# Attention and feed-forward on one core: the first stage and the first chunk issued from a written list, with z in SBUF and the weight conversion's shifted word moved from PSUM to SBUF

## The chip, the cores and the metric

The kernel runs on one core of a Trainium2 chip. The metric is the device time of one execution in microseconds (us); less is better. The engines are called TensorE or PE (matrix products), VectorE or DVE, ScalarE or ACT, GpSimd or POOL, and SyncE or SP (which here only issues DMAs). Each works through its own instructions in order; between engines there are semaphores.

## What is computed

Attention with a window of 16 and with one summary key and value for each block of 32 positions, then a two-layer feed-forward part with ELU, all in fp32:

```python
B, H, S, D = 4, 8, 768, 64;  block, window = 32, 16;  nb = S // block      # 24 blocks
k_sum = k.reshape(B, H, nb, block, D).max(axis=3)
v_sum = v.reshape(B, H, nb, block, D).mean(axis=3)
scores_l = where(|i - j| < window, scale * q @ k.T, -1e9)
scores_s = scale * einsum('bhsd,bhnd->bhsn', q, k_sum) + log(block)
a = softmax(concatenate([scores_l, scores_s]))          # denominator + 1e-9
x = (a @ concatenate([v, v_sum])) as [3072, 512]
out = elu(x @ w_in) @ w_out                              # 512 -> 2048 -> 512
```

## The kernel before

Queries are handled in windows of 64 with their 96 neighbouring keys and the 24 summaries: 120 columns of scores. A *third* is 256 queries of one batch element, a *pair* two heads; a *unit* is one third of one pair, a *group* two units. The rows of x (3072) are taken in six chunks of 512. Every fp32 product of the feed-forward part is three products of split operands: x, the weights and the activations are each kept as a high part (fp32r) and the rest. Layer 1 of one of the 16 slices f of the hidden dimension is 12 products of 512 columns, layer 2 likewise 12; one f of one chunk is a *step* n, of 24 products.

The weights arrive as 64-bit floats and are converted on the chip, 32 tiles of 128x512, two for each step of chunk 0. `convert` has five instructions on three engines: POOL cuts the low word's top bits (L103), ACT rescales the high word into a PSUM tile `sh` (L108), DVE shifts and joins (L110, in place in `sh`) and puts the sign on (L113, into the SBUF tile `cv`, two buffers), ACT makes the high part (L117), POOL subtracts to get the rest (L118). The ELU is an exp on ACT (L597), a min and add on DVE in SBUF (L601), a max and add on DVE with one operand in PSUM (L602), the split's high part on ACT (L608) and its rest `gl` on POOL (L609).

`first_units` is the first stage: scores, softmax and values for the first two thirds of batch element 0, pair by pair, which give chunk 0 its x. `exp` there writes the sums z into free columns of the score banks; pairs 0 and 2, and 1 and 3, share banks (L284). The means of v are products with a matrix `mean` over the loaded windows and over a second load of the last rows, `rest` (`sums`); `spread` copies them to `vsx` and broadcasts them by two DMAs on ACT's queue into the rows of `v_t` that `vals` reads. Behind it the loop over the 16 steps of chunk 0 interleaves layer 1, the conversions of the next weights, the units of the following two thirds one by one (with block-diagonal queries `qbd`, their windows of k and v loaded again), and layer 2 of the step before. In both, the order of instructions on every engine is the order of the program (`manual_schedule` for all five). From chunk 1 on, units go in groups, with a period of four steps: scores and softmax in step 0, transposes in 1 and 2, values in 2; there only PE's and SP's order is the program's, and a planner orders the other engines. PSUM has banks o0 to o3 (layer 2's sums), h (two buffers, layer 1), a0 and a1 (attention, conversion).

Of the kernel before, what the change touches and what calls it, by code (L numbers as in the profile page):

```python
# [26 lines left out]
P = 128  # L27
# [7 lines left out]
NEG = -1.0e9  # L35


@with_exitstack
def attn_elu_ffn(ctx: ExitStack, tc: tile.TileContext, qT, kT, vT, v, w_in, w_out, out):
# [37 lines left out]
    todo, loads = list(order), list(order)  # L77
# [13 lines left out]
    def load_more(n):  # L91
        while loads and len(order) - len(loads) < n:
            load(loads.pop(0))

    def convert(tag="a1"):

        key = todo.pop(0)  # L100
        raw = raws.pop(key)
        lo_w, hi_w = raw[:, :, 0], raw[:, :, 1]
        nc.gpsimd.tensor_scalar(out=lo_w, in0=lo_w.bitcast(U8)[:, :, 3], scalar1=1 / 32, scalar2=-31 / 64,  # L103
                                op0=ALU.mult, op1=ALU.add)
        yield
        sh = psum.tile([P, WC], F32, tag=tag, name="sh")
        bits = sh.bitcast(U32)
        nc.scalar.mul(out=sh, in_=hi_w.bitcast(F32), mul=2.0 ** -112)  # L108
        yield
        nc.vector.scalar_tensor_tensor(out=bits, in0=bits, scalar=3, in1=lo_w,  # L110
                                       op0=ALU.logical_shift_left, op1=ALU.bitwise_or)
        cv = ffn.tile([P, WC], F32, tag="cv", name="cv", bufs=2)
        nc.vector.scalar_tensor_tensor(out=cv.bitcast(U32), in0=hi_w, scalar=0x80000000, in1=bits,  # L113
                                       op0=ALU.bitwise_and, op1=ALU.bitwise_or)
        yield
        w = wts.tile([P, 2, WC], F32R, tag=f"w{key[0]}_{key[1]}", name=f"w{key[0]}_{key[1]}")
        nc.scalar.copy(out=w[:, 0, :], in_=cv)  # L117
        nc.gpsimd.tensor_tensor(out=w[:, 1, :], in0=cv, in1=w[:, 0, :].bitcast(F32), op=ALU.subtract)  # L118
        weights[key] = w
# [21 lines left out]
    def normalize(sm, got, z=None):  # L141
        z = got if z is None else z
        nc.vector.tensor_scalar(out=z, in0=got, scalar1=1e-9, scalar2=None, op0=ALU.add)
        nc.vector.reciprocal(out=z, in_=z)  # L144
        nc.gpsimd.tensor_tensor(out=sm, in0=sm, in1=z.broadcast_to([P, UW, KC]), op=ALU.mult)  # L145

# [6 lines left out]
    def values(v_t, w0, pt, tag=None, o_ps=None):  # L153
        if o_ps is None:
            o_ps = psum.tile([P, UT], F32, tag=tag, name="o_ps")
        for t in range(UW):
            for h in range(2):
                nc.tensor.matmul(o_ps[h * D:(h + 1) * D, t * QW:(t + 1) * QW],
                                 v_t[0:KC, w0 + t, h * D:(h + 1) * D], pt[0:KC, t, h * QW:(h + 1) * QW],
                                 start=True, stop=True)  # L160
        return o_ps

# [4 lines left out]

    def take_x(o_ps, third, p):
        xh, xl = xs[third // 2]
        cols = slice(third % 2 * UT, (third % 2 + 1) * UT)  # L170
        nc.scalar.copy(out=xh[:, p, cols], in_=o_ps)  # L171
        nc.vector.tensor_tensor(out=xl[:, p, cols], in0=o_ps, in1=xh[:, p, cols].bitcast(F32), op=ALU.subtract)  # L172
# [12 lines left out]
    spares = {}  # L185

    def first_units():
# [6 lines left out]
        W2 = 2 * UW  # L194
        free = [f"w{i}_{f}" for f in range(NF - 1, 0, -1) for i in (2, 1)]

        def borrow(shape, name):
            return wts.tile(shape, F32, tag=free.pop(0), name=name)

        spares[0], spares[1] = free[0:4], free[4:8]  # L200
        sms = [borrow([P, 2, UW, KC], f"sm{p}") for p in range(NP)]
        pts = [borrow([P, 2, UW, P], f"pt{p}") for p in range(NP)]
        kn = [borrow([P, E + S], f"kn{p}") for p in range(NP)]
        qn = [borrow([P, 2, CH], f"qn{j}") for j in range(2)]
        rest = borrow([P, 2, row], "rest")
        mean = borrow([P, 2, 2 * BLK], "mean")
        vsx = borrow([P, NP, P], "vsx")
# [49 lines left out]
        for i in range(2):  # L257
            nc.gpsimd.memset(qbd[i], 0.0)

        for p in range(NP):  # L260
            nc.gpsimd.memset(kw[p][:, UW - 1, KB - E:KB], 0.0)
            nc.gpsimd.memset(vw[p][QW:KB, UW - 1, :], 0.0)

        src = v[0]
        nc.sync.dma_start(out=v_t[0][E:KB, 0, :], in_=src[0:KB - E, :])
        for w0, w1 in ((1, UW), (UW, W2)):
            windows = bass.AP(tensor=src.tensor, offset=src.offset + (w0 * QW - E) * row,
                              ap=[[row, KB], [QW * row, w1 - w0], [1, row]])
# [12 lines left out]
        def scores(p):  # L281
            q_p = qn[p // 2][:, p % 2]
            for h in range(2):
                banks_of[p, h] = psum.tile([P, UW * P], F32, tag=f"o{(2 * p + h) % NSUB}", name="s")  # L284
            views = [banks_of[p, h][:, 0:UW * KC].rearrange("p (t k) -> p t k", k=KC) for h in range(2)]
            for cols in (slice(0, KB), slice(KB, KC)):
                for w in range(W2):
                    for h in range(2):
                        rows, half = slice(h * D, (h + 1) * D), slice(w % 2 * QW, (w % 2 + 1) * QW)
                        right = kn[p][rows, w * QW:w * QW + KB] if cols.start == 0 else ks[rows, p, :]  # L290
                        nc.tensor.matmul(views[h][half, w // 2, cols], q_p[rows, w * QW:(w + 1) * QW], right,  # L291
                                         start=True, stop=True)
# [76 lines left out]
        for p in range(NP):  # L369
            put_maxima(0, p)  # L370
# [446 lines left out]
```

## Time and profile before

| | |
|---|---|
| time, median of 3 runs | 662.15 us (659.97 to 663.66) |
| time of the profiled execution | 663.22 us |
| its span in the profile | 661.5 us |
| mean granted TensorE clock | 0.971 of full |
| TensorE products, busy | 632.8 us (96%) |
| VectorE, ScalarE, GpSimd busy | 269.1, 275.2, 243.0 us |

The times are those of whole executions; the profile is of one of them. In rows of instruction groups, "x96" is the number of instructions, and a name after "<-" behind an idle time says what ended it. A matmul of fp32 operands (not fp32r) shows as two records. Durations of neighbouring products overlap, so the start-to-start distance is what one costs.

### The profile page before, as it was taken

To read this page: it belongs to the slowest core of one execution; us is meant where nothing else is said; L and a number is where in the kernel's file an instruction comes from. 1 tells how busy PE (TensorE), PEld (TensorE's weight loads), DVE (VectorE), ACT (ScalarE), POOL (GpSimd) and SP (SyncE) were. 2 spreads that over 40 slices of the span, in tenths; PEclk is the share of its full clock that TensorE was granted. 3 is DMA by queue.
4 is the path that set the end of the run, shared out by engine and by line. 5 is a ranking of instruction groups with operands and counts; after the bars stand their busy time and mean duration, and the time that the engine had idled before them with its cause. 6 is when DMAs were issued, how large, how long until landed. Compare 5 with 4: busy or idle time off the path is not lost.

```text
span 661.5 us, 11268 instructions
## 1 busy us (share of the span) xinstructions
PE 632.8 (96%) x4204; PEld 511.4 (77%) x4204; DVE 269.1 (41%) x858; ACT 275.2 (42%) x746; POOL 243.0 (37%) x260
## 2 busy tenths in 40 slices
PE   6685999999999999999999999999999999999997
PEld 4564887887888887788888887888888888888885
DVE  5547887773333452432343353332423323322222
ACT  5346765773442442533433434434524424322222
POOL 4317896984331332232322322313313313222221
PEclk8676999999999999999999999999999999999999
DMA  9649856941310441422015222311311000100001
GB/s 279 171 127 283 291 163 176 270 129 40 103 42 25 134 110 47 143 65 60 1 50 145 88 66 69 103 50 31 110 39 39 24 1 1 64 0 1 0 1 63
DMA packets 70606, 59.62 MB, mean 90 GB/s; under 512 B 29224, under 2 KB 62312, under 8 KB 70552
## 3 DMA queue, kind: packets, MB, share of 16 engines
q1 hardware_dynamic: 67024, 52.61, 27.3%
q10 hardware_dynamic: 3528, 6.29, 2.7%
q8 instruction: 33, 0.54, 0.3%
q14 instruction: 21, 0.17, 0.1%
HBM read 51.41 MB, written 6.29 MB: 87 GB/s over the span
## 4 chain that ended last, share of the span: by engine, by line
PE 87%; DVE 4%; DMA 2%; POOL 1%; ACT 1%; issue 1%; SPq 0%; ACTq 0%; DVEq 0%; POOLq 0%
PE o L619 38%; PE h L591 38%; PE t_ps L150 3%; PE o_ps L561 3%; PE s L537 2%; PE o_ps L313 1%; DVE cv L113 1%; DVE sh L110 1%; DVE sm L129 1%; POOL w L118 1%; DMA kn<-in_kT_dram 1%; PE s L291 1%; PE vsps L330 1%; DMA vxl<-vsx 1%; DMA out_dram<-ot 1%
## 5 line engine op out<-in xcount | busy, mean ns | idle before, releaser
L591 PE MATMUL h<-xh,w 128*128 128x512 f32 x760 | 256.3, 398 | 0.0
L609 POOL TENSOR_TENSOR gl<-e,gh 128x512 fp32r<-128x512 f32 x96 | 123.8, 1290 | 332.9 <-ACT gh L608 239.6
L619 PE MATMUL o<-w,gh 128*128 128x512 f32 x768 | 198.4, 397 | 1.3 <-ACT ot L640 1.0
L591 PEld LDWEIGHTS h<-xh,w 128*128 128x128 f32 x760 | 143.8, 189 | 30.5
L619 PEld LDWEIGHTS o<-w,gh 128*128 128x128 f32 x768 | 140.7, 188 | 33.4 <-ACT e L597 2.2
L591 PE MATMUL h<-xl,w 128*128 128x512 f32 x380 | 149.1, 392 | 0.0
L601 DVE TENSOR_SCALAR e<-e 128x512 f32<-128x512 f32 x96 | 46.5, 484 | 251.4 <-ACT e L597 251.2
L597 ACT ACTIVATE e<-h 128x512 f32<-128x512 f32 x96 | 57.3, 597 | 186.6 <-PE h L591 183.7
L619 PE MATMUL o<-w,gl 128*128 128x512 f32 x384 | 105.5, 390 | 0.0
L608 ACT CAST gh<-e 128x512 fp32r<-128x512 f32 x96 | 59.5, 620 | 104.8 <-DVE e L602 104.8
L619 PEld LDWEIGHTS o<-w,gl 128*128 128x128 f32 x384 | 72.0, 188 | 15.6 <-POOL gl L609 0.2
L591 PEld LDWEIGHTS h<-xl,w 128*128 128x128 f32 x380 | 72.1, 190 | 13.7
L137 ACT ACTIVATE sm<-sm,mx 128x120 f32<-128x120 f32 x192 | 73.5, 386 | 15.9 <-DVE mx L129 7.0
L602 DVE SCALAR_TENSOR_TENSOR e<-h,e 128x512 f32<-128x512 f32 x96 | 66.4, 692 | 3.3
L145 POOL TENSOR_TENSOR sm<-sm,z 128x480 f32<-128x480 f32 x48 | 47.4, 987 | 45.9 <-DVE z L144 43.8
L118 POOL TENSOR_TENSOR w<-cv,w 128x512 fp32r<-128x512 f32 x32 | 42.1, 1316 | 13.0 <-ACT w L117 12.2
L150 PE MATMUL t_ps<-ident,sm 128*120 128x128 f32 x192 | 31.9, 295 | 10.9 <-DVE mx L129 7.8
L129 DVE CUSTOM_DVE_ANT_0 sm<-s,mask 128x120 f32<-128x120 f32 x192 | 41.1, 277 | 0.2
L150 PEld LDWEIGHTS t_ps<-ident,sm 128*120 128x120 f32 x192 | 25.1, 147 | 17.6 <-POOL raw_w L103 6.9
L172 DVE TENSOR_TENSOR xl<-o_ps,xh 128x256 fp32r<-128x256 f32 x40 | 16.9, 423 | 51.6 <-ACT xh L171 51.6
L137 ACT ACTIVATION_READ_ACCUMULATOR sm<-sm,mx 128x1 f32 x192 | 35.1, 183 | 0.0
L171 ACT CAST xh<-o_ps 128x256 fp32r<-128x256 f32 x40 | 14.8, 371 | 38.0 <-PE o_ps L561 28.4
(89 smaller groups left out, 378.3 us busy)
## 6 DMA issues: line engine op xcount, KB each, us to landing
raw_w<-in_w_in_dram SPq DMA_DIRECT2D x16, 512.0 KB
raw_w<-in_w_out_dram SPq DMA_DIRECT2D x16, 512.0 KB
out_dram<-ot ACTq DMA_DIRECT2D x20, 256.0 KB
qbd<-in_qT_dram SPq DMA_DIRECT2D x16, 256.0 KB
kw<-in_kT_dram SPq DMA_DIRECT2D x28, 144.0 KB
vw<-in_v_dram SPq DMA_DIRECT2D x28, 144.0 KB
n<-in_kT_dram SPq DMA_DIRECT2D x16, 192.0 KB
n<-in_vT_dram SPq DMA_DIRECT2D x16, 192.0 KB
```

What stands on the lines that cost most here:

```text
L118: nc.gpsimd.tensor_tensor(out=w[:, 1, :], in0=cv, in1=w[:, 0, :].bitcast(F32), op=ALU.subtract)
L129: nc.vector.tensor_tensor_reduce(out=sm[:, t, :], in0=s_ps[:, t, :], in1=m, scale=-scale, scalar=3.0e38, op0=ALU.add, op1=ALU.min, accum_o ...
L137: nc.scalar.activation(out=sm[:, t, :], in_=sm[:, t, :], func=AF.Exp, bias=mx[:, t, :], scale=-1.0, accum_out=z[:, t, :])
L145: nc.gpsimd.tensor_tensor(out=sm, in0=sm, in1=z.broadcast_to([P, UW, KC]), op=ALU.mult)
L150: nc.tensor.transpose(t_ps[0:KC, t, :], sm[:, t, :], ident)
L591: nc.tensor.matmul(h_ps, w[:, a, cols], bb[:, cc, :], start=(k == 0), stop=(k == 3 * NCC - 1))
L597: nc.scalar.activation(out=e, in_=h_ps, func=AF.Exp)
L601: nc.vector.tensor_scalar(out=e, in0=e, scalar1=1.0, scalar2=-1.0, op0=ALU.min, op1=ALU.add)
L602: top = nc.vector.scalar_tensor_tensor(out=e, in0=h_ps, scalar=0.0, in1=e, op0=ALU.max, op1=ALU.add)
L608: nc.scalar.copy(out=gh, in_=e)
L609: nc.gpsimd.tensor_tensor(out=gl, in0=e, in1=gh.bitcast(F32), op=ALU.subtract)
L619: nc.tensor.matmul(o_acc[c][s], a[:, s * P:(s + 1) * P], w[:, bb, :], start=first and f == 0, stop=last and f == NF - 1)
```

## The change

- **A written order.** The first stage and chunk 0 are cut into small functions, and a string `FIRST` of some 750 words names them one by one with their arguments (`do[name](*numbers)`). An engine's instructions come in the order in which the words that use it stand in the list.
- **First stage.** z is an SBUF tile; scores go to (o0, o1), (o2, o3), (a0, a1), (o0, o1); local and summary scores are separate words (`sl`, `ss`). `rest` is no longer loaded: all twelve windows of v of batch element 0 are, the last four into `v_own`, and the sums run over twelve windows. `vals` uses the 96 window rows only, and `add_means` adds the means by one product for each head of a pair. The DMAs that remain for the means (`vm`, on SP) fill `v_own` alone. Single idle products on zeros (`idle`) stand between the scores and the first transposes.
- **Groups in chunk 0.** The units of chunk 0 go as groups 0 to 3. Groups 0 and 1 (the last third of batch element 0) read k, the maxima and v from the tiles of the first stage; groups 2 and 3 load their windows. The scores and softmax of group 4 are in the list too.
- **Conversion.** `sh` is gone: ACT rescales into `cv` in SBUF (two buffers), and both joins work there in place.
- **Chunk 0's products.** Layer 1 is issued in two parts (8 and 4 products), layer 2 in three parts of 4.
- **Chunks 1 to 4.** A group's values go into a bank of h; the next group's scores and softmax move from its step 0 to step 2 of the group before; mean products for the next batch element come after layer 2 of their step.

```diff
+FIRST = """
+    max.0 sl.0 ss.0 low.0.0 max.1 exp.0.0 sl.1 low.0.1 ss.1 max.2 exp.0.1 low.1.0 sl.2 low.1.1 ss.2 idle.1
+    exp.1.0 max.3 sl.3 exp.1.1 z.0.0 z.0.1 low.2.0 ss.3 idle.1 norm.0.1 low.2.1 norm.0.0 tr.0.1 z.1.0 exp.2.1
+    sums.0 z.1.1 norm.1.0 low.3.0 tr.0.0 norm.1.1 low.3.1 exp.2.0 ptc.0.1.0 w.0 ptc.0.0.0 sums.1 exp.3.0 z.2.1
+    tr.1.1 z.2.0 w.1 norm.2.0 tr.1.0 ptc.1.1.0 val.0 exp.3.1 z.3.0 q.0 ptc.1.0.0 norm.3.0 sums.2 z.3.1 tr.2.0
+    norm.3.1 spr.0.0 spr.1.1 w.2 spr.2.1 val.1 spr.3.1 vm ptc.2.0.0 X.0 tr.3.0 norm.2.1 M.0 add.0 w.3 ptc.3.0.1
+    S.0 X.1 tr.2.1 xh.0 add.1 ptc.2.1.1 xl.0 w.4 H.0 tr.3.1 xh.1 L.0 val.2 ptc.3.1.0 M.1 sk.0 xl.1 val.3 X.2 q.1
+    S.1 M.2 add.2 X.3 S.2 add.3 w.5 xh.2 H.1 xl.2 first.0 xh.3 L.1 H.2 xl.3 w.6 first.1 L.2 first.2 M.3 S.3 sk.1
+    first.3 X.4 gsc.0 E.0 H.3 ts.0 X.5 w.7 M.4 stt.0 L1h.1 L.3 glow.0.0 G.0 glow.0.1 ge.0.0 X.6 w.8 L1l.1 S.4
...
+    H.17 L.17 L1l.8 glow.2.0 H.18 L.18 mmul glow.2.1 E.8 q.3 L2a.7 ts.8 ge.2.1 X.20 stt.8 L2b.7 X.21 w.25 L2c.7
+    G.8 gz.2.1 ge.2.0 L1h.9 gl.8 w.26 gn.2.1 M.19 gz.2.0 L1l.9 M.20 S.19 gn.2.0 mact mm w.27 L2a.8 E.9 S.20 H.19
+    L2b.8 L.19 w.28 L2c.8 ts.9 H.20 stt.9 L.20 gtr.2.0 L1h.10 gpc.2.0.1 w.29 G.9 M.21 gl.9 S.21 L1l.10 w.30 pm.3
...
+"""
+        def low_bits(self):                                            # X
+            nc.gpsimd.tensor_scalar(out=self.lo, in0=self.lo.bitcast(U8)[:, :, 3], scalar1=1 / 32, scalar2=-31 / 64,
+                                    op0=ALU.mult, op1=ALU.add)
+        def exponent(self):                                            # M
+            self.cv = ffn.tile([P, WC], F32, tag="cv", name="cv", bufs=2)
+            nc.scalar.mul(out=self.cv, in_=self.hi.bitcast(F32), mul=2.0 ** -112)
+        def join(self):                                                # S
+            bits = self.cv.bitcast(U32)
+            nc.vector.scalar_tensor_tensor(out=bits, in0=bits, scalar=3, in1=self.lo,
+                                           op0=ALU.logical_shift_left, op1=ALU.bitwise_or)
+            nc.vector.scalar_tensor_tensor(out=bits, in0=self.hi, scalar=0x80000000, in1=bits,
+                                           op0=ALU.bitwise_and, op1=ALU.bitwise_or)
+        def high(self):                                                # H
+            nc.scalar.copy(out=self.w[:, 0, :], in_=self.cv)
+        def rest(self):                                                # L
+            nc.gpsimd.tensor_tensor(out=self.w[:, 1, :], in0=self.cv, in1=self.w[:, 0, :].bitcast(F32),
+                                    op=ALU.subtract)
-        sh = psum.tile([P, WC], F32, tag=tag, name="sh")
-        nc.scalar.mul(out=sh, in_=hi_w.bitcast(F32), mul=2.0 ** -112)
...
+        tags = {0: ("o0", "o1"), 1: ("o2", "o3"), 2: ("a0", "a1"), 3: ("o0", "o1")}
-            z = banks_of[p, h][:, UW * KC:UW * KC + UW].rearrange("p (t o) -> p t o", o=1)
-            zs[p, h] = exps(sms[p][:, h], mxs[p, h], z)
+            zs[p, h] = exps(sms[p][:, h], mxs[p, h])
+        def add_means(p):
+            for h in range(2):
+                nc.tensor.matmul(o_of[p][h * D:(h + 1) * D].rearrange("p w q -> p (w q)"),
+                                 vsx[KB:KC, p, h * D:(h + 1) * D],
+                                 pts[p][KB:KC, h].rearrange("p t q -> p (t q)"), start=False, stop=True)
...
-        o_ps = psum.tile([P, 2, UT], F32, tag="a0", name="o_ps")
+        o_of[g] = psum.tile([P, 2, UT], F32, tag="h", name="o_ps", bufs=2)
...
+            if step == 2:
+                if g < NG:
+                    group_values(g)
+                if g + 1 < NG:
+                    group_scores(g + 1)
+                if g < NG:
+                    group_high(g)
+                    group_rest(g)
+                if g + 1 < NG:
+                    for h in range(2):
+                        softmax(g + 1, h)
```

The words: `max` maxima of k, `low` masked scores with their minimum, `z` sum plus 1e-9 and reciprocal, `norm` POOL's multiply by it, `tr` transposes, `ptc` their copy (0 on DVE, 1 on ACT), `val` values, `add` add_means, `xh`, `xl` the split of x; `first` the parts of layer 1 of f = 0; `w`, `q`, `K`, `sk`, `sv` loads; `gsc`, `glow`, `ge`, `gz`, `gn`, `gtr`, `gpc`, `gval`, `gxh`, `gxl` the same for groups; `L1h`, `L1l`, `L2a` to `L2c` the parts of the layers; `E`, `ts`, `stt`, `G`, `gl` the ELU and its split.

## Rows read from the trace of the kernel before

**Rows 1.** The page: busy time of the engines (share of the span, instructions), and TensorE's busy tenths in 40 equal slices.

```profile
PE 632.8 (96%) x4204; PEld 511.4 (77%) x4204; DVE 269.1 (41%) x858; ACT 275.2 (42%) x746; POOL 243.0 (37%) x260
...
PE   6685999999999999999999999999999999999997
```

**Rows 2.** The timeline, lines of the first stage and of the starts of step 1 and of chunk 1: start, duration, engine, line, what it writes and reads, and in brackets the idle time before it and what ended it.

```profile
4.99 0.89 PE L291 MATMUL s<-kn,qn 64*64 64x96 f32 x32
...
8.26 0.40 ACT L137 ACTIVATE sm<-sm,mx 128x120 f32<-128x120 f32 x1 [5.04 <-DVE mx L129]
...
12.45 1.39 PE L291 MATMUL s<-kn,qn 64*64 64x96 f32 x27 [1.63 <-DVE z L143]
...
20.11 1.39 PE L291 MATMUL s<-kn,qn 64*64 64x96 f32 x27 [2.02 <-DVE z L143]
...
33.57 0.39 ACT L137 ACTIVATE sm<-sm,mx 128x120 f32<-128x120 f32 x1 [2.34 <-DMA vxh<-vsx]
...
37.14 1.13 PE L313 MATMUL o_ps<-pt,vxl 120*64 120x64 f32 x16 [1.01 <-DMA vxl<-vsx]
...
57.77 1.08 PE L150 MATMUL t_ps<-ident,sm 128*120 128x128 f32 x4 [6.71 <-DVE mx L129]
58.51 0.78 PE L591 MATMUL h<-xh,w 128*128 128x512 f32 x1
...
160.39 0.50 PE L591 MATMUL h<-xl,w 128*128 128x512 f32 x1
```

**Rows 3.** Windows: stretch (us), its length, busy time and instructions of PE, PE's weight loads, DVE, ACT and POOL, granted clock, DMA share, GB/s. The first two are chunk 0 from step 1 on and all that follows.

```profile
58.44:160.46 102.02, 100.90 (x579) 81.81 (x578) 73.43 (x164) 64.78 (x157) 82.32 (x83) 0.98 0.64 196
160.46:661.50 501.04, 495.19 (x3096) 400.80 (x3096) 164.08 (x559) 183.10 (x496) 136.84 (x121) 1.00 0.19 56
...
0.00:20.00 20.00, 11.41 (x206) 7.94 (x206) 12.70 (x73) 10.23 (x43) 8.26 (x36) 0.79 0.96 282
...
80.00:100.00 20.00, 20.00 (x115) 16.65 (x114) 17.12 (x43) 12.82 (x29) 18.26 (x20) 1.00 0.56 186
120.00:140.00 20.00, 20.00 (x125) 16.40 (x124) 16.24 (x43) 13.86 (x34) 18.90 (x20) 1.00 0.85 246
```

**Rows 4.** Windows of 4 us in the first stage, same columns: the granted clock stands third from the end.

```profile
20.00:24.00 4.00, 3.89 (x78) 3.50 (x82) 0.66 (x2) 1.79 (x8) 1.82 (x5) 0.50 0.95 225
24.00:28.00 4.00, 4.00 (x77) 3.36 (x70) 2.05 (x19) 1.81 (x8) 0.99 (x1) 0.50 0.64 198
28.00:32.00 4.00, 2.04 (x12) 1.55 (x12) 2.45 (x8) 0.51 (x2) 1.65 (x2) 0.90 0.03 8
...
48.00:52.00 4.00, 2.07 (x17) 1.70 (x15) 2.02 (x11) 3.08 (x11) 2.22 (x3) 1.00 0.23 41
```

**Rows 5.** Groups of instructions by line and shape in the first 58 us: busy time, mean ns of one, idle time before and what ended it.

```profile
L137 ACT ACTIVATE sm<-sm,mx 128x120 f32<-128x120 f32 x36 | 14.0, 392 | 13.9 <-DVE z L143 5.7 <-DVE mx L129 5.0 <-DMA vxh<-vsx 2.3
...
L225 PE MATMUL idle<-kw 128*128 128x480 f32 x4 | 3.6, 1048 | 1.5 <-DVE kn L230 1.5
```

**Rows 6.** DMA issues by line: what is written from where, count, size of one.

```profile
raw_w<-in_w_in_dram SPq DMA_DIRECT2D x16, 512.0 KB
...
n<-in_kT_dram SPq DMA_DIRECT2D x4, 384.0 KB
```

**Rows 7.** The chain of work that ended last, pieces of one group's period in chunk 2: start, us, what.

```profile
279.02 2.75 PE o L619 x12
...
288.51 2.72 PE h L591 x12
...
304.27 2.75 PE o L619 x12
```

**Rows 8.** Single lines: durations of one instruction in ns (shortest/median/longest), first and last start, form.

```profile
L113 DVE SCALAR_TENSOR_TENSOR cv<-raw_w,sh x32: 686/687/690, 36.9 to 148.2; 128x512 uint32<-128x512 uint32 x32
...
L601 DVE TENSOR_SCALAR e<-e x96: 418/427/1551, 57.5 to 652.0; 128x512 f32<-128x512 f32 x96
...
L488 DVE TENSOR_REDUCE ks<-n x4: 922/934/954, 61.2 to 109.4; 128x24 f32<-128x768 f32 x4
...
L144 DVE RECIPROCAL z<-z x48: 177/178/179, 10.4 to 550.2; 128x4 f32<-128x4 f32 x48
...
L118 POOL TENSOR_TENSOR w<-cv,w x32: 1269/1293/1580, 39.0 to 151.6; 128x512 fp32r<-128x512 f32 x32
```

**Rows 9.** The timeline, a POOL instruction and a DVE instruction that starts during it.

```profile
71.71 1.29 POOL L118 TENSOR_TENSOR w<-cv,w 128x512 fp32r<-128x512 f32 x1
...
71.93 1.36 DVE L601 TENSOR_SCALAR e<-e 128x512 f32<-128x512 f32 x1
```

**Rows 10.** Groups of instructions by line from 58.5 to 153.5 us: busy time, mean ns, idle time before.

```profile
L118 POOL TENSOR_TENSOR w<-cv,w 128x512 fp32r<-128x512 f32 x29 | 38.3, 1320 | 3.6 <-ACT w L117 2.8
...
L609 POOL TENSOR_TENSOR gl<-e,gh 128x512 fp32r<-128x512 f32 x15 | 19.4, 1296 | 6.2 <-ACT gh L608 5.6
L110 DVE SCALAR_TENSOR_TENSOR sh<-sh,raw_w 128x512 uint32<-128x512 uint32 x27 | 18.8, 695 | 11.3 <-ACT sh L108 6.3 <-POOL raw_w L103 2.8 <-POOL w L118 1.5
L113 DVE SCALAR_TENSOR_TENSOR cv<-raw_w,sh 128x512 uint32<-128x512 uint32 x27 | 18.6, 687 | 7.1 <-POOL w L118 5.1
L103 POOL TENSOR_SCALAR raw_w<-raw_w 128x512 uint32<-128x512 uint8 x26 | 17.4, 670 | 5.2 <-DMA raw_w<-in_w_out_dram 3.0
...
L145 POOL TENSOR_TENSOR sm<-sm,z 128x480 f32<-128x480 f32 x7 | 6.9, 988 | 0.0
```

More of the change, by code (lines that the diff above doesn't have):

```diff
@@ L151, in transposes @@
         return t_ps
[L153 to L161, printed above, removed]
     xs = {}
@@ L279, in maxima, with scores @@
                                     axis=AX.X, op=ALU.max)
-        def scores(p):
+        tags = {0: ("o0", "o1"), 1: ("o2", "o3"), 2: ("a0", "a1"), 3: ("o0", "o1")}
+        value_tags = ("o2", "o3", "o0", "o1")
+        sums_of, t_of = [], {}
+        def scores(p, part):
             q_p = qn[p // 2][:, p % 2]
[L283 to L292, printed above, removed]
@@ L371, in first_units @@
-        scores(3)
-        trans(1, 0, dve)
-        low(3, 0)
-        norm(2, 0)
-        exp(3, 0)
-        low(3, 1)
-        ps = sums()
-        trans(1, 1, dve)
-        norm(2, 1)
-        spread(ps)
-        one = convert(tag="a1")
-        next(one)
-        exp(3, 1)
-        trans(2, 0, dve)
-        norm(3, 0)
-        next(one)
-        trans(2, 1, act)
-        next(one)
-        norm(3, 1)
-        trans(3, 0, dve)
-        vals(0, "a0")
-        list(one)
-        take(0)
-        two = convert(tag="o2")
@@ L435, in load_group, with low, exp @@
-    def load_group(g):
+                    rows, half = slice(h * D, (h + 1) * D), slice(w % 2 * QW, (w % 2 + 1) * QW)
+                    right = ks[rows, p, :] if part else kn[p][rows, w * QW:w * QW + KB]
+                    nc.tensor.matmul(banks_of[p, h][half, w // 2, cols], q_p[rows, w * QW:(w + 1) * QW], right,
+                                     start=True, stop=True)
+        def low(p, h):
+            mxs[p, h] = lowest({0: 0}, banks_of[p, h], sms[p][:, h])
+        def exp(p, h):
+            zs[p, h] = exps(sms[p][:, h], mxs[p, h])
@@ new lines, in spread, with all_means, first @@
+        def spread(p, copy):
+            copy(out=vsx[KB:P, p, :], in_=sums_of[0][p * BLK:(p + 1) * BLK, :])
+        def all_means(queue, tile_, n):
+            src = vsx[KB:KC].rearrange("n p (o d) -> n o (p d)", o=1)
+            queue.dma_start(out=tile_[KB:KC, :, :], in_=src.broadcast_to([NS, n, row]))
+        layer = []
+        def first(part):
+            xh, xl = xs[0]
+            w = weights[(1, 0)]
+            if not layer:
+                layer.append(new_h(0))
+            todo_ = {0: [(cc, 0, x) for cc in (0, 1) for x in (xh, xl)], 1: [(2, 0, xh), (2, 0, xl)],
+                     2: [(cc, 1, xh) for cc in (0, 1, 2)], 3: [(3, 0, xh), (3, 1, xh), (3, 0, xl)]}[part]
+            for i, (cc, a, x) in enumerate(todo_):
+                nc.tensor.matmul(layer[0], w[:, a, cc * P:(cc + 1) * P], x[:, cc, :],
+                                 start=(part, i) == (0, 0), stop=(part, i) == (3, 2))
@@ new lines, in first_units @@
+        copies = (nc.vector.tensor_copy, nc.scalar.copy)
+        parts = (range(0, UW), range(UW, W2), range(W2, W2 + UW))
+        return {
+            "max": maxima, "sl": lambda p: scores(p, 0), "ss": lambda p: scores(p, 1), "low": low, "exp": exp,
+            "z": recip, "norm": norm, "tr": trans, "ptc": lambda p, h, i: take_t(p, h, copies[i]), "val": vals,
+            "add": add_means, "xh": take_h, "xl": take_l, "sums": lambda i: sums(parts[i]), "first": first,
+            "spr": lambda p, i: spread(p, copies[i]), "idle": idle,
+            "vm": lambda: [all_means(nc.sync, tile_, 2) for tile_ in v_own],
+        }
```

562 lines of the change are left out of this document (250 added, 312 removed).

## The prediction, made before the changed kernel was run

> **What bounds the kernel now.** I read the page first: TensorE (PE) is busy 96% of the span, and its slices are thin only at the start [rows 1]. Then stages: the first layer-1 product of step n=1 starts at 58.51 us, the first of chunk 1 at 160.4 [rows 2], so the span has three stretches: a first stage of 58.5, the rest of chunk 0 of 102, and chunks 1 to 5 of 501. In the second PE is busy 100.9 of 102.0, in the third 495 of 501 [rows 3]: both are set by PE's own work. The reader should see two more things. GpSimd (POOL) is nearly full beside PE while weights are converted, 18.3 and 18.9 of 20 us in two stretches [rows 3]; afterwards it idles. And the first stage has no full engine: there PE waits, for z to be read out of a score bank (1.63 and 2.02), for the means that go by DMA (1.01), and 6.71 before step 1; ScalarE (ACT) stands 2.34 behind its own DMA issue [rows 2]. TensorE's clock is at half there for long stretches [rows 4].
>
> **First stage.** The change takes away all four waits: z lies in SBUF, pair 2 has banks a0 and a1, the means are added by products of their own, so values need no DMA, and the last exps no longer stand behind DMA issues. What is left is ACT's chain. Eight softmaxes are four exps each, and an exp with its accumulator read takes 0.39 plus some 0.1 [rows 5]; before, four took 1.81 (8.26 to 10.07). From about 7.4 (the first low no longer stands behind the second maximum) eight take 14.5, to 22. VectorE's (DVE) work ahead of the last low is four maxima of 0.94, eight lows of 0.82 and some z, under 13 us from 4.65, so ACT sets it. Before, the last exp ended at 35.5. Behind 22 us PE has in its order a third of the sums, four transposes, three value sets, four adds and the twelve products of the first layer. At full clock: 0.9 + 4 x 0.36 + 3 x 1.1 + adds + 2.7; at half: 1.8 + 4 x 1.0 + 3 x 1.7 + adds + 4.8. No row has an add (24 rows deep, 512 columns, fp32, two halves); from 0.45, two records like those of the first layer, to 1.8, half of the two idle products that took 3.57 [rows 5]. I take 0.85 at full and 1.7 at half, since a pair's halves can run side by side as the small score products do. Sums: 11.7 and 22.5, so layer 1 of f=0 would end between 34 and 45. The clock rose at 28 after PE had been busy from 20 to 28 [rows 4]; the new order keeps PE supplied from 14 on, so it should rise part of the way: I take 40. The count n=1 then starts 18 us earlier.
>
> Hidden there: 48 instead of 40 mean products (eight more are 0.4 to 0.9 on PE, inside the wait for exps), the larger load of v (736 instead of 512 KB, under 1 us at the 282 GB/s of the first 20 us [rows 3]; the 4.8 MB of the first loads end near 18, before the third sums are due), the extra memsets (before the first scores). Without that cover each costs what it takes. The queue of SP holds its weights behind the two DMAs of means until about 27; w.3 then lands near 32 and is wanted at about 40. Loads still to come are some 22 MB: 29 weights of 512 KB, eight summaries of 384, four groups of queries and three of windows [rows 6]; at 186 to 282 GB/s [rows 3] they take 78 to 118 us, less than what follows.
>
> **Chunk 0 on PE.** Twelve products take 2.72 us [rows 7]. Fifteen steps are 15 x 5.44 = 81.6. A group of two units costs 25.25 - 8 x 2.72 = 3.5 [rows 7]: four are 14.0; the split scores of groups 0 and 1 add 0.8, group 4's early scores 1.0, the mean products 0.4. Sum 97.8, against the 102.0 there was. If PE still set the pace, chunk 1 would start at 40 + 98 + 2 = 140 instead of 160.4. Splitting layer 1 and layer 2 into parts adds no product.
>
> **Chunk 0 on the other engines.** One edit looks free and decides, I think: the conversion's shifted word moves from a PSUM bank (sh) to SBUF (cv). Before, each of the two join instructions had one operand in PSUM; now all operands of both lie in SBUF, and so do those of POOL's subtracts and multiplies. What the trace shows of DVE beside a busy POOL: every instruction with a PSUM operand keeps its time to the nanosecond (the second join 686/687/690); the ELU's first half, all in SBUF, spreads from 418 to 1551 [rows 8]. One of them starts 0.22 after a POOL subtract and ends 0.29 after that ends [rows 9]. POOL too has its stretched ones (the subtract's median is 1293, its longest 1580). So DVE and POOL exclude each other for some all-SBUF instructions. Not for all: reductions (922 to 954) and the reciprocal (177 to 179) never stretch [rows 8]. No DVE instruction of the trace reads two SBUF tensors. So the price of a join beside POOL lies between 0 (like the reduction) and full exclusion (like the ELU's first half). I take the latter: it is elementwise, the same 128x512 fp32, and the joins differ from the undisturbed rows by the lost PSUM operand alone.
>
> The Trainium skill, page "SBUF — State Buffer", section "Who interferes with whom", says that a DVE instruction with two SBUF inputs contends with a GpSimd instruction that reads SBUF, the later one blocked until the other ends; no run here shows that for two inputs. By it the sum below stands at its upper end; without it chunk 0 costs PE's 98.
>
> Exclusive time from 40 us on, by the durations of chunk 0 [rows 10]: POOL 27 low-bit instructions x 0.670 + 28 subtracts x 1.32 + 15 gl x 1.296 + 8 multiplies x 0.988 = 82.4; DVE 29 joins x (0.695 + 0.687) + 15 x 0.427 = 46.5. Together 129, well over PE's 98. Some of each instruction's head can hide behind the other's tail (0.43 ended 0.29 after POOL: 0.14 a handover, some 60 handovers, 9 us): 120. The other way, both engines work in a listed order, the subtract waits for the joins through ACT, and in some turns neither has work ready; a sixth more gives 150. I take 134, nearer the sum: about 9 us a step. In that list ACT stands behind late joins with its exps, and PE behind ACT; PE would be busy three quarters of the time, as in 44 to 52, where the clock stayed at full [rows 4]; if it fell, more is lost.
>
> **Sum.** Chunk 1 at 40 + 134 = 174 instead of 160.4: +13.6. Chunks 1 to 5: the same products except group 4's scores, -1.0. The profiled execution took 663.22 with a span of 661.5: 675.8. The median of the runs is 1.07 lower: 674.7, I say 675. Bounds: 35 + 120 gives 657, 45 + 150 gives 697.
>
> **Rivals.**
> - *No exclusion for two inputs; PE sets the pace.* For: reductions read SBUF undisturbed. Then -20.4 - 1.0: 642; with the first layer at 35 or 45, 636 to 648. It decides as soon as joins cost POOL less than about a quarter of their time: 82 + 6 + a quarter of 40 is 98.
> - *Faster, but held by cv's two buffers.* The buffer is now taken by ACT's multiply, before the joins, and given back by POOL's subtract: 0.63 + 1.38 + 0.62 + 1.32 = 4.0, two at once 2.0 for each conversion, where PE's pace leaves 3.25. With waits in three listed queues a life could reach 7, then 3.5 each, +8 over 30 conversions: 650.
> - *Chunks 1 to 4 lose.* Values now take one of the two h banks, and the next group's scores and exps come in the same step. If ACT took the eight exps (8 x 0.38) ahead of the copies, the bank would be free about 5.6 us after the scores, when the layer that wants it is due at 5.5. Two us late in 16 groups is 32: from 642 to 674; it decides above 1.3 a group. Against: the copies stand ahead of the softmax in the program.
>
> **Chances.** The forecast 0.62 (its own range 658 to 690), no exclusion 0.24, cv's buffers 0.08, the later loop 0.06. The runs before spread over 0.56%, so 0.5% (3.3 us) is what a measurement can tell from no change. Slower: 0.56 of the forecast and 0.05 of the last, 0.61. Same: 0.07. Faster: the two faster rivals and the forecast's lowest end, 0.32. Since cases of both signs hold most of the chance, the range spans both: 638 to 692 leaves out some 0.1 on each side.
>
> **What would show it.** Right: the first layer's products end near 40 (34 to 45) with no z or DMA waits; both joins spread above 0.69, up to about 2; POOL's subtracts too; chunk 1 starts at 165 to 185 with PE gaps in chunk 0 released by ACT, DVE or POOL; from there about 500 to the end. Wrong: joins at a flat 0.69, PE gapless from 40 to 140. The forecast also fails if POOL's order leaves DVE its turns only in POOL's idle time, or if the clock falls in the gaps.

## The result and the profile after

The changed kernel takes 663.97 us (median of 20 runs, 662.05 to 672.09), the kernel before beside it 661.50 (20 runs): a ratio of 1.0058, 95% interval 1.0031 to 1.0086. Slower, by 2.5 us where 13 were forecast. The profiled execution took 664.48, its span is 662.7. Five of the 20 runs took 671 to 672, at a mean granted clock of 0.972 to 0.974 where the profiled one has 0.984; none of the five was profiled.

Windows of the changed kernel, cut where its last product of the first layer of f=0 ends and where chunk 1 starts; columns as in [rows 3]:

```profile
0.00:38.82 38.82, 32.30 (x548) 21.54 (x548) 27.86 (x118) 22.38 (x82) 19.26 (x50) 0.96 0.87 265
38.82:166.94 128.12, 106.19 (x753) 82.39 (x753) 111.30 (x205) 71.15 (x177) 99.20 (x87) 0.93 0.50 158
166.94:662.70 495.76, 490.65 (x3069) 401.93 (x3067) 159.92 (x540) 179.90 (x488) 141.47 (x122) 1.00 0.19 55
```

And its timeline, the first products of step n=1 and of chunk 1:

```profile
40.08 0.50 PE L596 MATMUL h<-xh,w 128*128 128x512 f32 x1
...
166.94 0.39 PE L585 MATMUL h<-xh,w 128*128 128x512 f32 x1
```

Cut at these two starts, the three stretches were 58.5, 101.9 and 501.1 [rows 2]; now they are 40.1, 126.9 and 495.8: -18.4, +25.0 and -5.3, which is, up to rounding, the 1.2 between the two spans. A gain and a loss of some 20 us each stand behind a result near zero. In chunk 0 PE is busy 106 of 128 us where it was busy 100.9 of 102; POOL works 99, DVE 111.

Single lines of the changed kernel (shortest/median/longest ns), to be held against [rows 8]: both joins, the ELU's second half, which takes one operand from PSUM, its first half, which has one input, in SBUF, and POOL's two conversion instructions.

```profile
L144 DVE SCALAR_TENSOR_TENSOR cv<-cv,raw_w x32: 677/1138/1798, 27.3 to 162.3; 128x512 uint32<-128x512 uint32 x32
L146 DVE SCALAR_TENSOR_TENSOR cv<-raw_w,cv x32: 691/1018/1669, 28.0 to 163.0; 128x512 uint32<-128x512 uint32 x32
L608 DVE SCALAR_TENSOR_TENSOR e<-h,e x96: 690/692/692, 41.4 to 653.6; 128x512 f32<-128x512 f32 x96
L605 DVE TENSOR_SCALAR e<-e x96: 394/427/1126, 40.5 to 653.2; 128x512 f32<-128x512 f32 x96
L155 POOL TENSOR_TENSOR w<-cv,w x32: 1267/1297/1742, 31.3 to 164.8; 128x512 fp32r<-128x512 f32 x32
L135 POOL TENSOR_SCALAR raw_w<-raw_w x32: 653/974/1149, 23.7 to 157.5; 128x512 uint32<-128x512 uint8 x32
```

The same two joins took 695 and 687 ns in chunk 0 while their shifted word lay in PSUM [rows 10]; now they spread to 1.8 and 1.7 us, while the ELU's second half, with h in PSUM, stays at 692. The second join is the cleaner comparison: it differs from before by one input, which moved from PSUM to SBUF; it took 686 to 690 ns there [rows 8] and takes 691 to 1669 here. How the two engines take turns stands in the timeline, POOL's lines first and then DVE's of the same stretch:

```profile
92.45 1.29 POOL L618 TENSOR_TENSOR gl<-e,gh 128x512 fp32r<-128x512 f32 x1 [0.33 <-ACT gh L613]
93.83 0.97 POOL L135 TENSOR_SCALAR raw_w<-raw_w 128x512 uint32<-128x512 uint8 x1
...
92.50 1.80 DVE L144 SCALAR_TENSOR_TENSOR cv<-cv,raw_w 128x512 uint32<-128x512 uint32 x1
94.33 1.01 DVE L146 SCALAR_TENSOR_TENSOR cv<-raw_w,cv 128x512 uint32<-128x512 uint32 x1
```

POOL's gl ends at 93.74; the join that started 0.05 after it ends 0.56 after that, at 94.30; POOL's low-bit instruction, begun meanwhile, ends 0.50 after the join, at 94.80; the next join 0.54 after that. In this stretch each gets on only when the other has ended. The Trainium skill's page "SBUF — State Buffer", section "Who interferes with whom", says this of a DVE instruction with two SBUF inputs beside a GpSimd instruction that reads SBUF; the trace agrees.

What waited in chunk 0 (waits from 38.8 to 167: total, times, longest):

```profile
ACT w L152 <- DVE cv L146: 34.0, 23, 3.7
POOL w L155 <- ACT w L152: 14.2, 14, 3.6
PE vsps L482 <- DVE mx L166: 7.6, 1, 7.6
PE o L628 <- ACT gh L613: 6.7, 4, 2.2
PE o L628 <- POOL gl L618: 3.6, 7, 1.3
```

ACT stands behind the joins for 34 us, POOL behind ACT, PE behind both: the order of waits that the prediction wrote down, though PE's largest single one is for DVE's masking of a group's scores (mx). The chain of work that ended last runs, in chunk 0, mostly along DVE's queue up to 107.7 us and again from 131 to 153, with the joins as its largest part; between 107.8 and 125.9 it is PE's products. Its pieces (start, us, what) around PE's wait of 7.6:

```profile
102.64 1.77 DVE cv L144
...
104.43 1.63 DVE cv L146
...
107.83 0.66 PE vsps L482 x8
108.48 4.96 PE o L628 x12
113.44 2.72 PE h L596 x12
```

The twelve products behind the wait took 4.96 us and the next twelve 2.72: from 104 to 112 the granted clock was 0.50, the lower level of 1.2 GHz, after PE had stood idle for 7.6 us.

### The profile page after: what moved, and what is told of

Same layout as the page of the kernel before. It is cut to its first block, busy times and chain, and to the rows that moved or that the text cites. A ratio compares the mean times of both kernels' runs of the same rounds, so it can differ in the third digit from the quotient of the medians.

```text
span 662.7 us, 11510 instructions
## 1 busy us (share of the span) xinstructions
PE 629.1 (95%) x4368; PEld 505.9 (76%) x4368; DVE 299.1 (45%) x861; ACT 273.4 (41%) x745; POOL 259.9 (39%) x257
## 4 chain that ended last, share of the span: by engine, by line
PE 80%; DVE 11%; issue 3%; DMA 2%; ACT 2%; POOL 1%; SPq 0%; ACTq 0%; DVEq 0%
PE h L585 33%; PE o L638 33%; DVE cv L144 4%; DVE cv L146 3%; PE t_ps L192 3%; PE o_ps L549 3%; PE s L513 2%; PE o L628 2%; PE h L596 1%; DMA n<-in_kT_dram 1%; DVE e L605 1%; PE idle L256 1%; PE s L324 1%; DVE sm L166 1%; DMA out_dram<-ot 1%
## 5 line engine op out<-in xcount | busy, mean ns | idle before, releaser
L618 POOL TENSOR_TENSOR gl<-e,gh 128x512 fp32r<-128x512 f32 x96 | 126.9, 1322 | 286.7 <-ACT gh L613 210.2
L585 PEld LDWEIGHTS h<-xh,w 128*128 128x128 f32 x640 | 120.1, 188 | 27.2 <-issue 2.8
L638 PEld LDWEIGHTS o<-w,gh 128*128 128x128 f32 x648 | 120.2, 188 | 25.5 <-DVE ot L659 1.2
L585 PE MATMUL h<-xl,w 128*128 128x512 f32 x320 | 124.5, 389 | 0.0
L638 PE MATMUL o<-w,gl 128*128 128x512 f32 x324 | 89.4, 390 | 0.0
L183 POOL TENSOR_TENSOR sm<-sm,z 128x480 f32<-128x480 f32 x40 | 44.9, 1124 | 69.1 <-DVE z L180 50.2
L638 PEld LDWEIGHTS o<-w,gl 128*128 128x128 f32 x324 | 60.7, 188 | 13.1 <-POOL gl L618 0.5
L585 PEld LDWEIGHTS h<-xl,w 128*128 128x128 f32 x320 | 60.2, 188 | 11.4
L174 ACT ACTIVATE sm<-sm,mx 128x120 f32<-128x120 f32 x160 | 60.9, 383 | 15.5 <-DVE mx L166 15.5
L144 DVE SCALAR_TENSOR_TENSOR cv<-cv,raw_w 128x512 uint32<-128x512 uint32 x32 | 35.8, 1120 | 10.6 <-ACT cv L140 7.6
L146 DVE SCALAR_TENSOR_TENSOR cv<-raw_w,cv 128x512 uint32<-128x512 uint32 x32 | 36.7, 1147 | 1.1
L628 PEld LDWEIGHTS o<-w,gh 128*128 128x128 f32 x120 | 23.9, 205 | 13.7 <-ACT gh L613 8.4
```

The source lines that it names most:

```text
L146: nc.vector.scalar_tensor_tensor(out=bits, in0=self.hi, scalar=0x80000000, in1=bits, op0=ALU.bitwise_and, op1=ALU.bitwise_or)
L174: nc.scalar.activation(out=sm[:, t, :], in_=sm[:, t, :], func=AF.Exp, bias=mx[:, t, :], scale=-1.0, accum_out=z[:, t, :])
L585: nc.tensor.matmul(h_ps, w[:, a, cols], bb[:, cc, :], start=(k == 0), stop=(k == 3 * NCC - 1))
L618: nc.gpsimd.tensor_tensor(out=gl, in0=e, in1=gs[(c, f)][0].bitcast(F32), op=ALU.subtract)
L628: nc.tensor.matmul(o_acc[0][s], gs[(0, f)][a][:, s * P:(s + 1) * P], w[:, bb, :], start=(f, part) == (0, 0), stop=False)
L638: nc.tensor.matmul(o_acc[c][s], a[:, s * P:(s + 1) * P], w[:, bb, :], start=first and f == 0, stop=last and f == NF - 1)
```

## The experiments

The theory after the result: chunk 0 is long because joins and POOL's instructions shut each other out, and the later loop is short because a group's small products stand in one run. Rivals: cv's two buffers, the list's order itself, and something that chunk 0 leaves to the later loop. Where a kernel before is named, it is the one timed on the same chip.

**Joins with one input in SBUF.** In the changed kernel, each join becomes a reduction of the same size that reads cv alone; buffers, order and POOL's work stay. The edit also takes away DVE's wait for POOL's low bits, which in the changed kernel comes once in chunk 0 and lasts 2.8 us.

```
-            bits = self.cv.bitcast(U32)
-            nc.vector.scalar_tensor_tensor(out=bits, in0=bits, scalar=3, in1=self.lo, ...)
-            nc.vector.scalar_tensor_tensor(out=bits, in0=self.hi, scalar=0x80000000, in1=bits, ...)
+            one = self.cv.rearrange("p (n k) -> p n k", k=1)
+            for _ in range(2):
+                nc.vector.tensor_reduce(out=self.cv, in_=one, axis=AX.X, op=ALU.max)
```

> The changed kernel with each of the two joins of a conversion replaced by a reduction over an axis of one: the same 128x512 tile in cv, the same places in the list, but one SBUF input instead of two. It leaves the joins' arithmetic out, so its weights are not the reference's. Theory (a join with two SBUF inputs and a GpSimd instruction shut each other out): the reductions take a flat 0.65 to 0.7 us beside GpSimd, chunk 0 (step 1 to chunk 1) falls from 127 to 98 to 106 us, time 636 to 645. Rival 1 (cv is held from ScalarE's multiply to GpSimd's subtract by two buffers) and rival 2 (the written list itself stalls, in whatever memory the joins read): both are unchanged here, chunk 0 stays above 118, time 655 to 664.

Measured: 636.24 us in the profiled execution and 647.50 in the only other one, the kernel before 660.85. Its reductions, as a single line, and the window of its chunk 0 (n=1 starts at 37.47):

```profile
L145 DVE TENSOR_REDUCE cv<-cv x64: 656/686/690, 26.0 to 132.5; 128x512 f32<-128x512 f32 x64
```

```profile
37.50:138.70 101.20, 98.01 (x692) 79.15 (x689) 81.61 (x207) 71.51 (x183) 85.55 (x85) 0.98 0.62 200
```

Beside a POOL that is busy 85.6 us of 101, 64 reductions spread over 34 ns in all. Chunk 0 takes 101.2, of which PE is busy 98.0, the 97.8 that the prediction gave PE. The cv buffers and the list are as they were, so neither alone held the changed kernel; joins that POOL shuts out cost it 126.9 - 101.2 = 25.7 us (PE's lower clock in the gaps included), all that chunk 0 lost. The run changes the kind of instruction together with the number of inputs. That it is the input in SBUF that matters rests on the second join before and after the change, not on this run; the ELU's first half, with one input, is stretched too (394 to 1126 ns).

**The kernel before with that one edit.** The shifted word moves from PSUM to cv; nothing else of the change.

```
-        sh = psum.tile([P, WC], F32, tag=tag, name="sh")
+        sh = cv = ffn.tile([P, WC], F32, tag="cv", name="cv", bufs=2)
...
-        cv = ffn.tile([P, WC], F32, tag="cv", name="cv", bufs=2)
```

> The kernel before with one edit: the shifted word sh lies in SBUF, in cv itself, instead of a PSUM bank; order, units and first stage as before. Theory: its joins spread from 0.69 to means of 1.0 to 1.2, the stretch from step 1 to chunk 1 grows from 102 to 122 to 130 us, time 682 to 692. Rival 2 (the loss comes from the written list): within 4 us of the kernel before, 658 to 667. Rival 1 (cv's two buffers): slower too, but with joins at 0.69 and waits of ScalarE for GpSimd's subtract.

Measured: 684.31 us, a ratio of 1.0354 (1.0306 to 1.0403); the span of the profile is 680.7, 19 us above the 661.5 of the kernel before. Step 1 to chunk 1 takes 123.3 (57.15 to 180.47) where it took 101.9. Time and stretch came as expected, the joins did not. Groups by line from 57 or 58 to 165 us (busy, mean ns, idle before and what ended it):

```profile
L112 DVE SCALAR_TENSOR_TENSOR cv<-raw_w,cv 128x512 uint32<-128x512 uint32 x26 | 19.6, 752 | 0.9
L110 DVE SCALAR_TENSOR_TENSOR cv<-cv,raw_w 128x512 uint32<-128x512 uint32 x26 | 18.8, 724 | 24.4 <-ACT cv L108 24.4
L600 DVE TENSOR_SCALAR e<-e 128x512 f32<-128x512 f32 x13 | 17.7, 1361 | 0.0
```

```profile
L608 POOL TENSOR_TENSOR gl<-e,gh 128x512 fp32r<-128x512 f32 x13 | 22.2, 1709 | 11.5 <-ACT gh L607 11.5
```

```profile
L108 ACT ACTIVATE cv<-raw_w 128x512 f32<-128x512 f32 x26 | 17.5, 674 | 45.9 <-POOL w L117 45.2
```

Joins of 0.73 us are hardly stretched: whoever comes second pays, and in this order that is POOL's gl (1709 in place of 1296 [rows 10]) and the ELU's first half (a mean of 1361 in place of 727 between 58.5 and 153.5 us of the kernel before). The joins come late for another reason: ACT waits 45 us for POOL to give a cv buffer back, DVE 24 for ACT. Joins near 0.69 and these waits are what rival 1 expected. So in this kernel the 21 us are not exclusion alone: the buffers, now held from ACT's multiply on, have a part in it that the run doesn't separate. In the changed kernel the same wait (ACT's multiply for POOL's subtract) is 5.8 us.

**POOL's subtract on DVE.** In the changed kernel, the subtract for a weight's rest goes to DVE; POOL keeps low bits, gl and multiplies.

```
-            nc.gpsimd.tensor_tensor(out=self.w[:, 1, :], in0=self.cv, in1=..., op=ALU.subtract)
+            nc.vector.tensor_tensor(out=self.w[:, 1, :], in0=self.cv, in1=..., op=ALU.subtract)
```

> The changed kernel with the subtract that makes a weight's rest moved from GpSimd to VectorE, at the same places of the list. Theory, by the sum of exclusive time: 29 subtracts of 1.32 on GpSimd become 29 of 0.69 on VectorE, 18 us less of it, chunk 0 at 108 to 113 us, time 644 to 652. Rival 3 (VectorE's own queue is the bound, busy 110 of 127 us, not the shared port): 20 us more for VectorE, chunk 0 at 130 to 147, time 667 to 684.

Measured: 663.54 us, 1.0042 of the kernel before (1.0019 to 1.0064): no change from the changed kernel's 1.0058. The window of its chunk 0, in an execution of 670.63, and its three largest groups on DVE there (busy, mean ns, idle before):

```profile
48.20:171.60 123.40, 103.97 (x694) 80.90 (x690) 113.01 (x225) 68.51 (x170) 56.44 (x53) 0.93 0.43 133
```

```profile
L146 DVE SCALAR_TENSOR_TENSOR cv<-raw_w,cv 128x512 uint32<-128x512 uint32 x28 | 27.8, 992 | 1.0
L144 DVE SCALAR_TENSOR_TENSOR cv<-cv,raw_w 128x512 uint32<-128x512 uint32 x28 | 26.8, 958 | 4.4 <-POOL raw_w L135 2.8 <-issue 1.5
L155 DVE TENSOR_TENSOR w<-cv,w 128x512 fp32r<-128x512 f32 x29 | 23.2, 803 | 1.7 <-ACT w L152 1.5
```

The same two joins in the changed kernel, from 38.8 to 167:

```profile
L146 DVE SCALAR_TENSOR_TENSOR cv<-raw_w,cv 128x512 uint32<-128x512 uint32 x29 | 34.3, 1182 | 1.0
L144 DVE SCALAR_TENSOR_TENSOR cv<-cv,raw_w 128x512 uint32<-128x512 uint32 x29 | 33.4, 1152 | 10.4 <-ACT cv L140 7.4 <-POOL raw_w L135 2.8
```

POOL's load falls from 99 to 56 us, yet the whole time stays and this chunk 0 is only 3.5 us shorter. By the sum of exclusive times (129 - 28 x 1.32 + 28 x 0.69 = 111) 18 us should have come back, so that sum alone doesn't set the chunk. DVE's queue suggests why: with less of POOL beside them 28 pairs of joins take some 11 us less, but the subtracts add 23.2, and DVE is busy 113.0 us where it was busy 110.1. Its instructions with PSUM operands stand in that queue too. Neither expectation held.

**No low bits.** In the changed kernel, POOL's 28 low-bit instructions are left out; the join reads the high word twice, still two SBUF inputs.

```
-            nc.gpsimd.tensor_scalar(out=self.lo, in0=self.lo.bitcast(U8)[:, :, 3], ...)
...
-   nc.vector.scalar_tensor_tensor(out=bits, in0=bits, scalar=3, in1=self.lo, ...)
+   nc.vector.scalar_tensor_tensor(out=bits, in0=bits, scalar=3, in1=self.hi, ...)
```

> The changed kernel without POOL's instruction that makes the lowest three bits of a weight (28 of some 0.67 us each in chunk 0); the first join takes the high word in its place, so it still reads two inputs in SBUF, and the weights are not the reference's. The theory that a POOL instruction that reads SBUF and a join shut each other out, whatever the POOL instruction is, expects the 18.1 us of these instructions back nearly whole: chunk 0 in 108 to 112 us in place of 128, 644 to 650 in all. If only POOL's instructions with two inputs (the subtractions) shut the joins out, these 28 cost chunk 0 nothing: 660 to 666. If chunk 0 is held by DVE's own queue, as the run with the subtraction moved to DVE suggests, part comes back, 6 to 12 us: 652 to 658.

Measured: 655.3 us (9 runs), 0.9903 (0.9877 to 0.9929), 8.7 under the changed kernel. The profiled execution took 665.41, with n=1 only at 48.9; its chunk 0 ends at 167.8, 118.9 us, 8 less, with both joins still at 1039 and 1156 ns. Low bits do shut joins out (in the changed kernel they take 884 ns in chunk 0 where they took 670), but 18.1 us taken away return 8. The time came as in the third expectation. DVE is busy 102.4 us where it was busy 110.1, and the chunk fell by as much; but a busy DVE includes the time for which POOL shuts it out (with the unstretched reductions it is busy 81.6), so this is not a bound of DVE's work alone. POOL waits 28.8 us for ACT's high parts where it waited 14.2: part of the time taken from it became idle time.

**The later loop alone.** The kernel before, with the group's values in tag h and the next group's scores and softmax behind them.

```
-         o_ps = psum.tile([P, 2, UT], F32, tag="a0", name="o_ps")
+         o_ps = psum.tile([P, 2, UT], F32, tag="h", name="o_ps", bufs=2)
...
-            if g < NG and step == 0:
+            if g == G0 and step == 0:
...
+            if step == 2 and g + 1 < NG:
+                group_scores(g + 1)
```

> The kernel before with one part of the change alone, that of the loop over chunks 1 to 5: a group's products with v go to the tag h, and behind them at once stand the scores and the softmax of the next group, where they stood at the next group's first step. First stage, chunk 0 and the conversions are the kernel's before. The theory is that this alone gave the changed kernel its shorter later loop (501.1 us before, 495.8 after): one stretch of small products a group in place of two, so 0.2 to 0.3 us less a group, 15 groups (group 4's scores stay where they were), and about 1 us less at the unit that takes new weights of the mask: 656 to 659 us beside a kernel before of 661, a ratio of 0.993 to 0.997, with a group period of 25.0 in place of 25.25. The rival is that the 5 us come from what chunk 0 left behind (group 4's scores already done, and summaries already made): then this kernel takes the time of before, 660 to 662, and its group period stays at 25.25.

Measured: 657.05 us, 0.9948 (0.9925 to 0.9971), 3.8 under the kernel before. The starts of the values of two groups in a row, in the kernel before, in this one and in the changed one:

```profile
281.70 1.15 PE L561 MATMUL o_ps<-pt,vw 120*64 120x64 f32 x32
306.95 1.15 PE L561 MATMUL o_ps<-pt,vw 120*64 120x64 f32 x32
```

```profile
278.18 1.15 PE L561 MATMUL o_ps<-pt,vw 120*64 120x64 f32 x32
303.17 1.15 PE L561 MATMUL o_ps<-pt,vw 120*64 120x64 f32 x32
```

```profile
259.48 1.15 PE L549 MATMUL o_ps<-pt,vw 120*64 120x64 f32 x32
285.88 1.15 PE L549 MATMUL o_ps<-pt,vw 120*64 120x64 f32 x32
```

The first pair is 25.25 apart, the second 24.99. In place of two stretches of small products (values, scores) a group has one, and that is worth 0.26 us; 14 of the 15 periods between the first and the last group are shorter by 0.26 to 0.30, 3.8 us in all. Where the 0.26 lies shows in the chain of the kernel before, with values at 203.58 and scores at 213.05: the twelve products right behind either take 2.94 and 2.99, the next twelve 2.72.

```profile
204.66 2.94 PE h L591 x12
207.61 2.72 PE o L619 x12
...
214.03 2.99 PE o L619 x12
217.01 2.72 PE h L591 x12
```

The third pair spans the end of chunk 1, 26.40 apart, where the kernel before takes 27.68: PE waits there for the copies of the outputs, 1.3 us before and 0.5 in the changed kernel, but 1.6 in this run. So this edit doesn't make that second gain. Nor does the change's chunk 0: the version from both, below, has the kernel before's chunk 0 with the whole changed loop, and there the wait is 0.5 and the period 26.39. Which part of the rest makes it was not tried.

**A version from both.** It keeps the change's first stage and later loop and takes the kernel before's chunk 0: join through a PSUM bank, the units' attention between the layers.

```
+            sh = psum.tile([P, WC], F32, tag="a1", name="sh")
+            bits = sh.bitcast(U32)
+            nc.scalar.mul(out=sh, in_=hi_w.bitcast(F32), mul=2.0 ** -112)
...
+            nc.vector.scalar_tensor_tensor(out=cv.bitcast(U32), in0=hi_w, scalar=0x80000000, in1=bits, ...)
```

> The changed kernel's first stage (its list up to the first layer, joins in SBUF there), then the loop of the kernel before for chunk 0 (units one by one, sh in a PSUM bank), then the changed kernel's loop for chunks 1 to 5. Theory: step 1 starts at 40 to 44, chunk 0 takes 100 to 105, the rest 496 to 498, time 638 to 648, faster than both. Rival (the early start is lost again because fewer weights are converted and loaded ahead): chunk 0 above 115, time above 654.

Measured: 646.61 us, 0.9812 (0.9745 to 0.9879), with its second join at 686/689/691 ns again. In the profiled execution n=1 starts at 44.9, later than expected; chunk 0 takes 102.6 and the rest 496.1, as expected, so the early start is not lost again. PE stood idle for 4.6 us before n=1, for unit 0's multiplication on POOL, which stood in POOL's queue behind a conversion whose transfer landed at 37.8. Two more orders of the same work:

```
- X.3 S.2 add.3 us.0 ... ul.0 ue.0 w.6 first.1 L.2 first.2 M.3 S.3 uz.0 first.3 un.0
+ S.2 add.3 us.0 ... ul.0 ue.0 w.6 first.1 L.2 first.2 uz.0 un.0 X.3 M.3 S.3 first.3
```

> The version that keeps the change's first stage and its later loop and has before's chunk 0 (join in PSUM, the units' attention inside the chunk), with three steps of the list put in another order: the conversion of the fourth weight tile, whose transfer lands at 37.8 us, stood ahead of two subtractions on POOL that could have gone at 35 to 36, and unit 0's multiplication stood behind both, so that PE stood idle for 4.6 us before unit n=1. Now the two subtractions and the multiplication go first. The theory is that PE's wait of 4.6 shrinks to under 1, unit n=1 starts at 40 to 41 in place of 44.9 and the whole takes 639 to 643 us, 20 under before. The rival is that the wait only moves to the weights of n=2, which come by the late transfer: then 643 to 647.

```
+            h_ps = layer1(0, n)
+            if n == 1:
+                evacuate = unit_transposes(0)      # was at the end of n == 0
```

> As the version with the list put in another order (hybrid2), with one more step of PE's order changed: there PE still stood idle for 3.75 us before unit n=1, at the transposes of the first unit's softmax, since they write the PSUM bank from which DVE takes the next unit's scores only at 42. Here the products of unit n=1 go ahead of these transposes. The theory is that PE goes on at 38 to 39 in place of 42.4, the wait shrinks under 1 us, and an execution at the full clock takes 639.5 to 641, 3 to 4 us less than hybrid2's 643.8. The rival is that unit n=1 then waits for what follows, the ELU of unit 0 or the conversion of n=2's weights, whose transfer lands at 37.8, and the whole stays at 643 to 645.

Measured: 647.33 (0.9794, 0.9741 to 0.9846) and 646.35 (0.9820, 0.9771 to 0.9868). Neither order brought the gain that its theory expected: the wait moved, as both rivals said, though in the second not to the weights of n=2, and both medians lie above the rivals' ranges. PE's waits from 30 to 60 us, of the first order, the second and the third:

```profile
PE t_ps L163 <- POOL sm L154: 4.6, 1, 4.6
PE o L662 <- ACT gh L637: 1.1, 1, 1.1
```

```profile
PE t_ps L163 <- DVE mx L137: 3.7, 1, 3.7
PE o L662 <- ACT gh L637: 1.0, 1, 1.0
```

```profile
PE o L662 <- ACT gh L637: 5.1, 1, 5.1
PE t_ps L163 <- DVE mx L137: 1.0, 1, 1.0
```

The wait of 4 to 5 us changes its name, hardly its length. All three are about 14 us faster than the kernel before and 17 than the changed one.

## Why the prediction was right and wrong

**Right, in part by luck: the first stage.** "I take 40": the first layer ends at 38.8 and n=1 starts at 40.08, 18.4 earlier as written, and the last exp ended at 21.1 where 22 was expected. But 40 lay between 34 at full clock and 45 at half, and from 20 to 40 us the granted clock was 0.91. The sum behind the exps was too small: from 22.69 to 38.82 us that work took 16.1 us, where the sum at full clock had 11.7 (at full clock a pair's add took 1.0 in place of 0.85, four transposes 0.58 in place of 0.36, the first layer 3.3 in place of 2.7). A clock that was expected lower made up for it.

**Right: the mechanism of chunk 0.** With both inputs in SBUF the joins and POOL exclude each other; both spread to 1.7 and 1.8 ("up to about 2"), POOL's instructions stretch too, chunk 1 starts at 166.9 (within 165 to 185). The run with one-input reductions shows that this and not cv's buffers cost the 25 us: without it chunk 0 takes 101.2, with PE busy for the 98 of the prediction.

**Wrong: "I take 134, nearer the sum".** Measured: 126.9, from n=1 to chunk 1. The plain sum of exclusive times was 129; the 5 put on top of it for turns in which neither engine has work had no row, nor had the sixth that gave 150. The 0.14 that hides at each handover is there (0.50 to 0.56 of a 0.67 to 0.69 us instruction remain); that idle turns took back about what it saves would fit, but is not shown. That the sum came within 2 us is no law, and in part luck: two runs in which it fell by 18 gave back 0.4 and 8.7 us of the whole time. The chain shows what the sum leaves out: it runs along DVE's queue, busy 110.1 of 126.9 us, in which the shut-out joins stand together with instructions that exclude nothing, and from 107.8 to 125.9 along PE. The clock, which the prediction kept at full in the gaps, was granted 0.93 over chunk 0. How much of a step is exclusion and how much DVE's listed order stays open.

**Wrong: "Chunks 1 to 5: the same products except group 4's scores, -1.0".** Measured: -5.3. The same products in another order aren't the same time: one stretch of small products a group in place of two saves 0.26 or a little more, 3.8 in 14 periods. The numbers lay near [rows 7]: 25.25 less eight times 2.72 leaves 3.5 for a group's small products, where their own pieces in the chain make 2.9, and that rest was costed as fixed. The period at the end of chunk 1 gave 1.3 (0.8 of it a shorter wait for the outputs' copies), and the first group, whose scores were ready, 0.3 in place of 1.0.

The two terms are 7.1 and 4.3 us too dear; together they are the 11.3 between 675.8 and the profiled 664.48. The rival in which the later loop loses by the h bank is refuted: it gains.

## What to carry to other kernels

Before an operand moves from PSUM to SBUF, count how many SBUF inputs that leaves on its DVE instruction, and what POOL runs beside it: here joins that POOL shut out cost 25.7 us in chunk 0, more than a first stage made 18 us shorter brought in. When a loop that PE bounds is reordered, count the changes between small and full products, not the products alone. Where two engines exclude each other, a sum of exclusive times need not give the price of an edit: look also at what the edit adds to the queue along which the chain runs.

## What the runs showed of the hardware beyond that

Under exclusion the stretch falls on the instruction that comes second: with the same edit the joins' means are 1152 and 1182 ns in one order and 724 and 752 in the other, where POOL's gl and the ELU pay. A flat duration therefore doesn't show that an instruction takes no part.

One first stage ran at two clocks. In the changed kernel and in the one with the subtract on DVE, whose first stage differs by that alone, PE is busy alike in the first 20 us, at full clock; from 20 to 40 the granted clock is 0.91 in the one and 0.57, near the lower level of 1.2 GHz, in the other, and n=1 starts at 40.1 and 48.2. The windows, first of the changed kernel:

```profile
0.00:20.00 20.00, 15.85 (x344) 10.88 (x344) 16.24 (x99) 12.94 (x61) 8.68 (x39) 1.00 0.95 266
20.00:40.00 20.00, 17.63 (x270) 11.84 (x268) 12.76 (x21) 10.03 (x23) 11.66 (x13) 0.91 0.79 270
```

```profile
0.00:20.00 20.00, 15.92 (x347) 10.64 (x348) 16.81 (x100) 13.46 (x64) 9.19 (x39) 1.00 0.94 269
20.00:40.00 20.00, 18.23 (x187) 11.71 (x188) 9.92 (x17) 6.00 (x16) 8.44 (x12) 0.57 0.81 278
```

The run without low bits has 0.58 there and starts n=1 at 48.9. The two ends of the prediction's 34 to 45 were meant for these two clocks.
